# First units of a tile with attention turns between them, in a kernel of linear attention and two gated layers

## The chip, the cores and the metric

The kernel runs on one core of one Trainium2 chip. The metric is the device time of one execution in microseconds. The engines are named as the profile names them: PE is TensorE (matmul), PEld its weight loads, DVE VectorE, ACT ScalarE, SP SyncE, which here issues the DMAs, one behind the other in its own order.

## The reference

Random-feature attention on 4 batches of 8 heads, 576 tokens, 64 values a head (b h s d), with 128 features (m), then two layers over all 2304 tokens of 512 values:

```python
def phi(x):
    proj = np.einsum('bhsd,md->bhsm', x, omega)
    sq = np.sum(x * x, axis=-1, keepdims=True) / 2.0
    h = proj - sq
    h = h - np.max(h, axis=-1, keepdims=True)
    return np.exp(h) / np.sqrt(m)
q_p, k_p = (phi(q_s), phi(k_s))
kv = np.einsum('bhsm,bhsd->bhmd', k_p, v)
z = np.sum(k_p, axis=2)
num = np.einsum('bhsm,bhmd->bhsd', q_p, kv)
den = np.einsum('bhsm,bhm->bhs', q_p, z)[..., None] + 1e-06
attn_out = num / den
...
h = x @ w_in                                   # 512 -> 2048
x = (h * (1.0 / (1.0 + np.exp(-1.702 * h)))) @ w_out   # 2048 -> 512
...
a = x @ w_a                                    # 512 -> 1536
b = x @ w_b
return a * b @ w_out                           # 1536 -> 512
```

q_s and k_s are q and k by a constant. All is in float32.

## The kernel before

Most products are made of fp16 pairs: each float32 operand is split into a high and a low half, and high·high, high·low and low·high are summed, three matmuls for one product.

The first layer runs over five token tiles: one of 512 tokens for each batch, and one of 256 for the tokens left over. `ffn1` (L608 on) makes a tile of 16 units of 128 hidden values. A unit's h products are L623 to L625 (four chunks of 128 inputs, three matmuls of 512 columns each); then tanh on ACT (L631), `th` on DVE (L634), the high half `gh` on ACT (L640), the low half `gl` on DVE (L641); and the unit's 12 y products (L654 to L656) add into four accumulators, which are copied out at the tile's end (`ye`, ACT, L668) and stored. `main` runs y of unit f and then h of unit f + 2. The first units of a tile are made by `head`, before `main`: it issues the products of the first units on chunks 0 to 2, then, unit by unit, those on chunk 3 with all that follows. The input is xT; its chunk c is written by head pair c of the batch's attention, so that chunk 3 comes last.

Attention of one batch is a set of eight Python generators: four k phases (`kphase32`, L493; one pair of heads each) and four q phases (`qphase`, L513). A phase loads raw k or q, makes the fp16 pair x16 (ACT L394, DVE L395), transposes it by DMA into xt (L400), sums the squares (ACT L413 or L421, DVE L423), projects on omega (PE, L406 and L407), takes maxima (DVE L470) and small per-token terms (DVE L476), exponentials (ACT L437), and then the k phase forms kv (PE, L501 and L503). The q phase transposes the exponentials (PE L526, copied by ACT L528), multiplies by kv (PE L533), normalises (DVE L557 to L562, into xf), makes an fp16 pair again (ACT L595, DVE L596) and transposes it by DMA into xT (L603).

Weights arrive as raw chunks of 1 MB (`wraw`, L200, two buffers) and are split into halves by DVE (L214, L254, L262, L221) and ACT (L272), in steps: `w_steps(n, upto)` takes n of them, and one step issues the load of the chunk two further on.

The order of the program is written by four helpers. `begin_k` and `begin_q` put the phases into a list, each to start two turns behind the one before. `side_step` is one turn: every live phase goes on to its next yield. `run(gen, rate, wmax)` goes through a generator, and at each yield does `rate` steps of weight conversion and one turn. `finish_side` takes turns until no phase is left; `next_tile` calls it before the next tile is made. A scheduler then sets the order on each engine from dependencies and priorities, which follow the program's order. Attention of batch b runs beside tile b − 1 (its x is made by batch b − 1), and the q phase's end loads the next batch's k.

Batch 0's attention comes first, alone. Then `head(following[0], 3)` makes three units of tile 0 in one go (`following` is the list of tiles). Then, for b = 1, 2, 3: the phases of batch b are put on the list and the tile b − 1 is run with turns between. Behind batch 1's loop, `head(following[-1], 2)` makes two units of tile 1 in one go.

Of the kernel before, what the change touches and what calls it, by code (L numbers as in the profile page):

```python
# [33 lines left out]
def fused_kernel(  # L34
# [40 lines left out]
    first = ExitStack()  # L75
# [91 lines left out]
    NW1 = len(chunks)  # L167
# [117 lines left out]
    def w_steps(n, upto):  # L285
        for _ in range(n):
            if w_done[0] < upto:
                w_done[0] = next(w_gen)

    def w_need(n):  # L290
        while w_done[0] < n:
            w_done[0] = next(w_gen)
# [11 lines left out]
    def alloc_own(pool):  # L304


        own["ident"] = pool.tile([P, P], F32, name="ident", bufs=1)
        own["kv"] = pool.tile([P, NHP, 2, VC], F32, name="kv32", bufs=1)
        make_identity(nc, own["ident"])
        own["vt"] = vt = pool.tile([P, H, NT, VC], F32, name="vt", bufs=1)  # L310
        own["vm"] = vm = pool.tile([P, NHP, 2, VC], F32, name="vm", bufs=1)
        nc.gpsimd.memset(vt[:, :, :, D:VC], 1.0)
        nc.gpsimd.memset(vm, 0.0)
        for hh in range(2):
            nc.gpsimd.memset(vm[hh * SR : (hh + 1) * SR, :, hh, D:VC], 1.0)

    def prep(pool):
        om2 = stg.tile([P, 2, D], F32, tag="sx", name="om2", bufs=1)
        om = own["om"]
        for j in range(2):  # L320
            nc.vector.tensor_scalar(
                out=om2[:, j, :], in0=om, scalar1=QSCALE * S_OM, scalar2=None, op0=ALU.mult
            )
        pt = ps_att.tile([P, 512], F32, tag="att", name="pt")
        nc.tensor.transpose(pt[:, :P], om2.rearrange("p a b -> p (a b)"), own["ident"])
        nc.gpsimd.memset(om_f, 0.0)
        for j in range(2):
            nc.vector.tensor_copy(om_f[j * D : (j + 1) * D, j], pt[j * D : (j + 1) * D, :P])
        nc.scalar.copy(om_h, pt[:, :P])
        nc.vector.tensor_tensor(out=om_l, in0=pt[:, :P], in1=om_h, op=ALU.subtract)  # L330
# [6 lines left out]
    def a_load(pool, kind, b, hp):  # L337

        if b >= B or (kind, b, hp) in raws:
            return  # L340
        src = {"q": q, "k": k}[kind]
        h0 = 2 * hp
        place = kind
        if b == 0 and hp == NHP - 1:
            place = {"q": "k", "k": "q"}[kind]
        t = pool.tile([P, T, D], F32, tag=f"raw{place}", name=f"raw{kind}_{b}_{hp}", bufs=RAW[place])
        nc.sync.dma_start(
            out=t[:, 0 : 2 * NT, :].rearrange("p (h t) d -> p h (t d)", h=2),
            in_=src[b, h0 : h0 + 2, 0:SM, :].rearrange("h (p t) d -> p h (t d)", t=NT),
        )  # L350
        nc.sync.dma_start(out=t[:, 2 * NT, :], in_=src[b, h0 : h0 + 2, SM:S, :])
        raws[kind, b, hp] = t

    def v_load(b, part=None):
        if b >= B:
            return
        main = v[b, :, 0:SM, :].rearrange("h (p t) d -> p h t d", t=NT)
        for t in range(NT) if part is None else (part,):
            nc.sync.dma_start(out=own["vt"][:, :, t, 0:D], in_=main[:, :, t])
        for hh in (0, 1) if part is None else (part,) if part < 2 else ():  # L360
            nc.sync.dma_start(
                out=own["vm"][hh * SR : (hh + 1) * SR, :, hh, 0:D],
                in_=v[b, :, SM:S, :].rearrange("(n h) s d -> h s n d", h=2)[hh],
            )
# [633 lines left out]
    def side_step():  # L998

        while waiting and waiting[0][0] <= turn[0]:  # L1000
            live.append(waiting.pop(0)[1])
        for g in list(live):
            if next(g, live) is live:
                live.remove(g)
        turn[0] += 1
# [10 lines left out]
    def run(gen, rate, wmax):  # L1016

        due = 0.0
        for _ in gen:
            due += rate  # L1020
            if rate < 1:
                with tc.issue_after(own["nb"]):
                    w_steps(int(due), wmax)
            else:
                w_steps(int(due), wmax)
            due -= int(due)
            side_step()

    def finish_side():
        while waiting or live:  # L1030
            side_step()
# [7 lines left out]
    def begin_k(b, pool, psp, t0, lag, f32):  # L1039
        for hp in range(NHP):  # L1040
            def nx(hp=hp):
                if hp + 1 == NHP:
                    a_load(pool, "q", b, 0)

            begin(t0 + lag * hp, kphase32(pool, b, hp, psp, nx, f32))

    def begin_q(b, pool, xT, psp, t0, lag, f32):
        for hp in range(NHP):
            def nx(hp=hp):
                if hp + 1 < NHP:  # L1050
                    a_load(pool, "q", b, hp + 1)
                with tc.issue_after(own["xt", f"q{b}_{hp}"].ins):
                    a_load(pool, "k", b + 1, hp)
                if hp + 1 == NHP:
                    begin(0, v_parts(b + 1, own["xt", f"q{b}_{hp}"]))

            begin(t0 + lag * hp, qphase(pool, b, hp, xT, psp, nx, f32))

    def xparts(xT):
        return lambda c: xT[:, c, 0, :], lambda c: xT[:, c, 1, :]  # L1060

    def x_tile(b, pool, tag):
        return pool.tile([P, KC, 2, SM], F16, tag=tag, name=f"xT{b}")
# [4 lines left out]
    def fillers(n):  # L1068
        for _ in range(n):
            nc.tensor.matmul(  # L1070
                idle[:, 0:256].rearrange("p (r m) -> p r m", r=2), om_h,
                om_h[:, None, :].to_broadcast([P, 2, M]), start=True, stop=True,
            )
# [15 lines left out]
    following = []  # L1089

    def head(tile, units):
        _, products, unit = tile
        for f in range(units):
            w_need(2 * (f // RW) + 1)
            if f < 2:
                products(f, range(KC - 1))
            else:
                products(f, range(KC - 1), ps_acc, "acc")
        for f in range(units):
            unit(f, (KC - 1,))  # L1100

    def next_tile(make):
        def made():
            finish_side()
            following.append(make())
            return following[-1]

        return made

    xT = x_tile(0, zp, "z")  # L1110
    with tc.tile_pool(name="att", bufs=2) as att:
        own["om"] = att.tile([P, D], F32, tag="om", name="om", bufs=1)
        nc.scalar.dma_start(out=own["om"], in_=omega)
        a_load(att, "k", 0, 0)
        warm = att.tile([P, 1], F32, tag="warm", name="warm", bufs=1)
        nc.vector.memset(warm, 0.0)
        nc.scalar.activation(out=warm, in_=warm, func=AF.Exp)
        alloc_own(att)
        prep(att)
        fillers(1)  # L1120
        for hp in range(1, NHP):
            a_load(att, "k", 0, hp)
        w_steps(START_W, NW1)
        begin_k(0, att, psp_start, 0, LAG, True)
        begin_q(0, att, xT, psp_start, NHP * LAG, LAG, True)
        for n in range(VT):
            side_step()
        v_load(0)
        finish_side()
        fillers(FILL)  # L1130
        w_steps(POST_W, NW1)
        following.append(ffn1(0, *xparts(xT), SM))
        head(following[0], 3)
        for b in range(1, B):
            x1 = x_tile(b, zp, "z")
            begin_k(b, att, psp_att, 0, AL, b == 1)
            begin_q(b, att, x1, psp_att, NHP * AL, AL, b == 1)
            ahead = next_tile(lambda: ffn1(b, *xparts(x1), SM))
            if b == 1:
                run(following[-1][0](first=3), 1, NW1)  # L1140
                ahead()
                head(following[-1], 2)
            else:
                run(following[-1][0](ahead), 11 / 32, (NW1 + 2, NWE)[b - 2])
    late["pool"] = ctx.enter_context(tc.tile_pool(name="late", bufs=1))
    run(following[-1][0](next_tile(rest_tile)), 22 / 32, NW2)
# [48 lines left out]
```

## Time and profile before

| | |
|---|---|
| median of 3 runs | 915.58 us (915.47, 915.58, 917.74) |
| the profiled execution | 920.41 us |
| its span | 918.6 us |
| mean granted clock of TensorE | 0.994 |
| busy PE, PEld | 887.8 us (97%), 640.3 us (70%) |
| busy DVE, ACT | 678.5 us (74%), 440.2 us (48%) |
| y products, L655 | 115.2 us in 320, 4.7 us idle before them, by gl |
| h products, L623 | 97.9 us in 256, 4.3 us idle before them, 2.8 of it by xT |

Busy time is summed over the span. The profile was taken from one execution, and its span stands 1.8 us under that execution's time. Times in rows count from the start of the span; a group's idle time is that of its engine just before the group's instructions, with the releaser that ended most of it. Rows of TensorE overlap: a matmul's duration is longer than the time from its start to that of the next one. A row with "x22" stands for so many instructions, fp32 matmuls counting twice because they go through the array in two passes.

### The profile page before, as it was taken

The numbers are of one execution on the slowest core, as the hardware profiler recorded it, in microseconds if no ns is written. First come the engines' busy times: TensorE is split into PE (matmuls) and PEld (weight loads), VectorE is DVE, ScalarE is ACT, GpSimd is POOL, SyncE is SP. The second block draws the span as 40 slices with busy tenths as digits, with TensorE's granted clock in tenths as the row PEclk, the third lists the DMA queues.
The fourth block names the chain that finished last, engine by engine and source line by source line (L and its number), as shares of the span: only waits on it lengthen the run. The fifth ranks groups of instructions, "written<-read, shape, count | busy, mean of one in ns | idle before, by whom it ended". The sixth has DMA issues, their size and how long they took to land.

```text
span 918.6 us, 17124 instructions
## 1 busy us (share of the span) xinstructions
PE 887.8 (97%) x6984; PEld 640.3 (70%) x6984; DVE 678.5 (74%) x1220; ACT 440.2 (48%) x1047; POOL 1.7 (0%) x11
## 2 busy tenths in 40 slices
PE   7999989989999999999999999999999999999997
PEld 6864555645655456544447888888988888888886
DVE  5889988555779477899943379976999567566766
ACT  5656777554655566655423355443543232232221
POOL 0000000000000000000000000000000000000000
PEclk9999998999999999999999999999999999999999
DMA  7846686432475324773521043323330122223312
GB/s 178 222 129 193 201 211 177 140 62 72 115 155 137 92 61 66 133 215 127 211 92 46 1 145 101 124 103 118 131 127 16 67 42 81 81 93 127 76 47 70
DMA packets 129343, 105.35 MB, mean 115 GB/s; under 512 B 97776, under 2 KB 111088, under 8 KB 127216
## 3 DMA queue, kind: packets, MB, share of 16 engines
q1 hardware_dynamic: 128960, 103.96, 40.0%
q8 instruction: 55, 0.90, 0.4%
q10 hardware_dynamic: 304, 0.30, 0.1%
q14 instruction: 24, 0.20, 0.1%
HBM read 71.07 MB, written 17.69 MB: 97 GB/s over the span
## 4 chain that ended last, share of the span: by engine, by line
PE 65%; DVE 21%; ACT 6%; DMA 6%; issue 2%; SPq 1%; ACTq 0%; DVEq 0%
PE y L655 4%; PE y L656 4%; PE ph L623 4%; PE ph L625 4%; PE ph L624 4%; PE y L654 4%; PE pa L503 2%; PE oA L873 2%; PE oA L871 2%; PE oA L872 2%; PE pbA L778 2%; PE pbA L780 2%; PE pbA L779 2%; PE paA L778 2%; DVE wf L254 2%
## 5 line engine op out<-in xcount | busy, mean ns | idle before, releaser
L655 PE MATMUL y<-gl,w_out 128*128 128x512 f16 (+1 forms) x320 | 115.2, 361 | 4.7 <-DVE gl L641 4.7
L656 PE MATMUL y<-gh,w_out 128*128 128x512 f16 (+1 forms) x320 | 115.3, 361 | 0.0
L654 PE MATMUL y<-gh,w_out 128*128 128x512 f16 (+1 forms) x320 | 112.3, 358 | 0.1
L623 PE MATMUL ph<-xT,w_in 128*128 128x512 f16 x256 | 97.9, 382 | 4.3 <-DMA xT<-x_q_3x 2.8
L625 PE MATMUL ph<-xT,w_in 128*128 128x512 f16 x256 | 98.1, 383 | 0.6 <-DVE w_in L221 0.6
L624 PE MATMUL ph<-xT,w_in 128*128 128x512 f16 x256 | 97.6, 381 | 0.3 <-DVE xT L592 0.3
L634 DVE SCALAR_TENSOR_TENSOR th<-th,ph 128x512 f32<-128x512 f32 (+1 forms) x80 | 50.4, 630 | 47.9 <-ACT th L631 47.5
L631 ACT ACTIVATE th<-ph 128x512 f32<-128x512 f32 (+1 forms) x80 | 44.3, 553 | 62.6 <-PE ph L625 60.2
L640 ACT ACTIVATE gh<-th 128x512 f16<-128x512 f32 (+1 forms) x80 | 47.0, 588 | 52.3 <-DVE th L634 52.0
L641 DVE SCALAR_TENSOR_TENSOR gl<-th,gh 128x512 f16<-128x512 f32 (+1 forms) x80 | 50.6, 634 | 17.3 <-ACT gh L640 17.0
L778 PE MATMUL paA<-forms,w_a 128*128 128x256 f16 (+1 forms) x240 | 61.0, 262 | 1.6 <-DVE ca L797 0.8
L778 PE MATMUL pbA<-forms,w_b 128*128 128x256 f16 (+1 forms) x240 | 61.1, 262 | 1.0 <-DVE cb L797 1.0
L780 PE MATMUL pbA<-forms,w_b 128*128 128x256 f16 (+1 forms) x240 | 61.0, 262 | 0.0
L779 PE MATMUL pbA<-forms,w_b 128*128 128x256 f16 (+1 forms) x240 | 61.0, 262 | 0.0
L780 PE MATMUL paA<-forms,w_a 128*128 128x256 f16 (+1 forms) x240 | 61.0, 262 | 0.0
L779 PE MATMUL paA<-forms,w_a 128*128 128x256 f16 (+1 forms) x240 | 61.0, 262 | 0.0
L871 PE MATMUL oA<-w_o,ab 128*128 128x256 f16 x216 | 58.9, 273 | 1.6 <-ACT ab L829 0.9
L873 PE MATMUL oA<-w_o,ab 128*128 128x256 f16 x216 | 58.9, 273 | 0.6 <-DVE ab L830 0.5
L872 PE MATMUL oA<-w_o,ab 128*128 128x256 f16 x216 | 58.9, 273 | 0.0
L656 PEld LDWEIGHTS <-w_out 128*128 128x128 f16 x320 | 31.4, 98 | 35.2 <-issue 7.6
L624 PEld LDWEIGHTS <-w_in 128*128 128x128 f16 x320 | 31.7, 99 | 32.9 <-issue 6.1
L786 ACT COPY ka<-paA 128x512 f32<-128x512 f32 (+1 forms) x30 | 16.3, 544 | 78.2 <-PE paA L780 78.1
(195 smaller groups left out, 2317.5 us busy)
## 6 DMA issues: line engine op xcount, KB each, us to landing
wraw<-in_moe_w_out_dram SPq DMA_DIRECT2D x14, 1024.0 KB
forms<-fd SPq DMA_DIRECT2D x8, 1792.0 KB
wraw<-in_moe_w_in_dram SPq DMA_DIRECT2D x8, 1024.0 KB
fd<-forms SPq DMA_DIRECT2D x4, 1792.0 KB
wraw<-in_moe_w_a_dram SPq DMA_DIRECT2D x6, 1024.0 KB
wraw<-in_moe_w_b_dram SPq DMA_DIRECT2D x6, 1024.0 KB
rawk<-in_k_dram SPq DMA_DIRECT2D x16, 256.0 KB
vt<-in_v_dram SPq DMA_DIRECT2D x16, 256.0 KB
```

The costliest lines, as they stand in the source:

```text
L623: nc.tensor.matmul(ph[:, :n], w[:, 0, c, fs], xh(c), start=(c == 0), stop=False)
L624: nc.tensor.matmul(ph[:, :n], w[:, 0, c, fs], xl(c), start=False, stop=False)
L625: nc.tensor.matmul(ph[:, :n], w[:, 1, c, fs], xh(c), start=False, stop=(c == KC - 1))
L654: nc.tensor.matmul(o, w[:, 0, f % 4, cs], gh[f][:, :n], start=(f == 0), stop=False)
L655: nc.tensor.matmul(o, w[:, 0, f % 4, cs], gl[f][:, :n], start=False, stop=False)
L656: nc.tensor.matmul(o, w[:, 1, f % 4, cs], gh[f][:, :n], start=False, stop=(f == FC1 - 1))
L778: nc.tensor.matmul(o[:, i], wh, xh, start=first, stop=False, skip_group_check=True)
L779: nc.tensor.matmul(o[:, i], wh, xl, start=False, stop=False, skip_group_check=True)
L780: nc.tensor.matmul(o[:, i], wl, xh, start=False, stop=final, skip_group_check=True)
L871: nc.tensor.matmul(bank[:, t], lh, wh, start=first, stop=False, skip_group_check=True)
L872: nc.tensor.matmul(bank[:, t], lh, wl, start=False, stop=False, skip_group_check=True)
L873: nc.tensor.matmul(bank[:, t], ll, wh, start=False, stop=final, skip_group_check=True)
```

## The change

`head` becomes a generator with a yield behind each unit's first products and behind each unit. For batch 1, tile 0's head of three units is no longer issued ahead of the loop, but inside it, behind `begin_k` and `begin_q`, through `run` at one weight step and one turn a yield: six yields, six turns. Tile 1's head of two units moves from the end of the pass for b = 1 into that for b = 2, again behind `begin_k` and `begin_q`, through `run` at 11/32 weight steps a yield: four turns. The passes for b = 3 and for the rest stay.

```diff
                 products(f, range(KC - 1))
             else:
                 products(f, range(KC - 1), ps_acc, "acc")
+            yield
         for f in range(units):
             unit(f, (KC - 1,))
+            yield
...
         following.append(ffn1(0, *xparts(xT), SM))
-        head(following[0], 3)
         for b in range(1, B):
             x1 = x_tile(b, zp, "z")
             begin_k(b, att, psp_att, 0, AL, b == 1)
             begin_q(b, att, x1, psp_att, NHP * AL, AL, b == 1)
             ahead = next_tile(lambda: ffn1(b, *xparts(x1), SM))
             if b == 1:
-                run(following[-1][0](first=3), 1, NW1)
+                run(head(following[0], 3), 1, NW1)
+                run(following[0][0](first=3), 1, NW1)
                 ahead()
-                head(following[-1], 2)
             else:
+                if b == 2:
+                    run(head(following[-1], 2), 11 / 32, NW1 + 2)
                 run(following[-1][0](ahead), 11 / 32, (NW1 + 2, NWE)[b - 2])
```

How this moves instructions is shown at three places. In the order's names, `ph1_0` is tile 1's product of unit 0, `y0_1` tile 0's accumulator 1, `gh0_14` the high half of tile 0's unit 14, `xt_q1_2` the transposed q of batch 1, head pair 2; the numbers behind are the compiler's.

TensorE around the last attention product of batch 1 (L533, head pair 3), only matmuls' rows picked from the list, the weight loads (LDWEIGHTS) between them left away. The kernel before:

```order
L533 MATMUL pa_2084<-kv32_113,eT32_q1_3_2040 128x65 x4
L533 MATMUL pa_2084<-kv32_113,eT32_q1_3_2040 64x65 x2
L533 MATMUL pa_2120<-kv32_113,eT32_q1_3_2040 128x65 x5
L624 MATMUL ph1_1_2222<-xT1_911,w_in0_87 128x512
L625 MATMUL ph1_1_2222<-xT1_911,w_in0_87 128x512
L623 MATMUL ph1_0_2212<-xT1_911,w_in0_87 128x512
```

The same place in the changed kernel:

```order
L533 MATMUL pa_1966<-kv32_113,eT32_q1_3_1925 128x65 x4
L533 MATMUL pa_1966<-kv32_113,eT32_q1_3_1925 64x65 x2
L533 MATMUL pa_1995<-kv32_113,eT32_q1_3_1925 128x65 x5
L656 MATMUL y0_1_1011<-gh0_14_2134,w_out3_92 128x512
L654 MATMUL y0_2_1015<-gh0_14_2134,w_out3_92 128x512
L655 MATMUL y0_2_1015<-gl0_14_2135,w_out3_92 128x512
```

Before, tile 1's h products follow the last attention product at once, and the first on chunk 3 stands eight matmuls behind it. Now y products of tile 0's unit 14 follow, then those of unit 15 and tile 1's products on chunks 0 to 2: 37 matmuls up to the first on chunk 3.

SP's queue around the transposition of batch 1's second q, with the weight loads behind it. The kernel before:

```order
L200 DMA wraw12_1648<-in_moe_w_in_dram 128x4x512
L400 DMA_TRANSPOSE xt_q1_1_1398<-x16_q1_1_1395 128x9x128
L347 DMA rawk_2_1_1442<-in_k_dram 128x2x256
L351 DMA rawk_2_1_1442<-in_k_dram 128x1x64
L200 DMA wraw13_1700<-in_moe_w_out_dram 128x2x1024
L200 DMA wraw14_1883<-in_moe_w_in_dram 128x4x512
```

The same place in the changed kernel:

```order
L200 DMA wraw9_1467<-in_moe_w_out_dram 128x2x1024
L200 DMA wraw10_1642<-in_moe_w_in_dram 128x4x512
L400 DMA_TRANSPOSE xt_q1_1_1283<-x16_q1_1_1280 128x9x128
L347 DMA rawk_2_1_1324<-in_k_dram 128x2x256
L351 DMA rawk_2_1_1324<-in_k_dram 128x1x64
L200 DMA wraw11_1696<-in_moe_w_out_dram 128x2x1024
L400 DMA_TRANSPOSE xt_q1_2_1394<-x16_q1_2_1391 128x9x128
```

The transposition `xt_q1_1` was followed by weight chunk 13 and is now followed by chunk 11; chunk 9 follows `xt_q1_0`, chunk 12 follows `xt_q1_2` and chunk 13 follows `xt_q1_3`, in the same way.

SP's queue at the end of tile 0: stores of y, the last transpositions of batch 1's output into xT, the loads of k of batch 2, head pair 3, and its first transposition `xt_k2_0`. The kernel before:

```order
L669 DMA yd0_2199<-ye0_3_2209 128x512
L603 DMA_TRANSPOSE xT1_911<-x16_q1_1x_1994 128x8x128
L603 DMA_TRANSPOSE xT1_911<-x16_q1_2x_2078 128x8x128
L603 DMA_TRANSPOSE xT1_911<-x16_q1_3x_2148 128x8x128
L400 DMA_TRANSPOSE xt_k2_0_2273<-x16_k2_0_2270 128x9x128
L347 DMA rawk_2_3_1671<-in_k_dram 128x2x256
L351 DMA rawk_2_3_1671<-in_k_dram 128x1x64
```

The same place in the changed kernel:

```order
L603 DMA_TRANSPOSE xT1_841<-x16_q1_3x_2028 128x8x128
L669 DMA yd0_2199<-ye0_1_2203 128x512
L669 DMA yd0_2199<-ye0_2_2206 128x512
L669 DMA yd0_2199<-ye0_3_2209 128x512
L347 DMA rawk_2_3_1553<-in_k_dram 128x2x256
L351 DMA rawk_2_3_1553<-in_k_dram 128x1x64
L400 DMA_TRANSPOSE xt_k2_0_2227<-x16_k2_0_2224 128x9x128
```

The first transposition of batch 2 stood ahead of the loads of `rawk_2_3` and now stands behind them and behind three stores of y.

## Rows read from the trace of the kernel before

**Rows 1.** Busy time of each engine by stretch: us, PE PEld DVE ACT POOL, PEclk, DMA, GB/s.

```profile
59.00:192.00 133.00, 124.33 (x754) 68.96 (x751) 110.80 (x194) 85.25 (x300) 0.00 (x0) 0.97 0.61 170
...
60.00:120.00 60.00, 56.64 (x323) 29.08 (x322) 58.38 (x89) 40.40 (x152) 0.00 (x0) 1.00 0.63 183
...
138.00:144.00 6.00, 5.99 (x15) 2.08 (x15) 4.18 (x7) 4.99 (x25) 0.00 (x0) 0.51 0.47 116
...
195.00:199.00 4.00, 4.00 (x21) 2.28 (x20) 2.39 (x4) 3.28 (x6) 0.00 (x0) 0.57 0.78 171
...
200.00:918.00 718.00, 704.29 (x5844) 522.57 (x5841) 522.30 (x909) 311.17 (x624) 0.00 (x0) 1.00 0.34 98
```

**Rows 2.** Timeline of TensorE, mid-tile: start, us, instruction, [idle before].

```profile
138.01 0.59 PE L655 MATMUL y<-gl,w_out 128*128 128x512 f16 x1 [2.74 <-DVE gl L641]
...
143.93 0.38 PE L624 MATMUL ph<-xT,w_in 128*128 128x512 f16 x1
```

**Rows 3.** Chain of waits, 120 to 205 us: start, us, what.

```profile
123.71 1.96 SPq L400
...
127.02 7.57 DMA wraw<-in_moe_w_out_dram
134.61 0.70 DVE wf L214
...
137.36 0.61 DVE gl L641
```

**Rows 4.** Timeline of TensorE: matmuls and projections one behind another.

```profile
66.74 0.38 PE L623 MATMUL ph<-xT,w_in 128*128 128x512 f16 x1
66.96 0.38 PE L624 MATMUL ph<-xT,w_in 128*128 128x512 f16 x1
...
80.65 0.22 PE L406 MATMUL pa<-om_h,xt_k 128*128 128x128 f16 x1
80.70 0.22 PE L407 MATMUL pa<-om_l,xt_k 128*128 128x128 f16 x1
```

**Rows 5.** Timeline of TensorE, end of tile 0.

```profile
181.38 2.63 PE L533 MATMUL pa<-kv,eT_q 128*128 128x65 f32 x22 [0.54 <-ACT eT_q L528]
...
185.11 0.74 PE L526 MATMUL pa<-ident,e_q 128*128 128x128 f32 x5 [0.62 <-DVE xf_q L562]
...
186.54 2.53 PE L533 MATMUL pa<-kv,eT_q 128*128 128x65 f32 x22
...
190.54 0.38 PE L623 MATMUL ph<-xT,w_in 128*128 128x512 f16 x1 [1.04 <-DMA xT<-x_q_2x]
...
194.76 0.38 PE L623 MATMUL ph<-xT,w_in 128*128 128x512 f16 x1 [2.76 <-DMA xT<-x_q_3x]
...
198.60 0.38 PE L624 MATMUL ph<-xT,w_in 128*128 128x512 f16 x1
```

**Rows 6.** Chain of waits, 120 to 205 us, end of tile 0.

```profile
191.47 3.25 DMA xT<-x_q_3x
```

**Rows 7.** Timeline of VectorE, early in tile 0.

```profile
83.82 0.75 DVE L395 SCALAR_TENSOR_TENSOR x_k<-rawk,x_k 128x576 f16<-128x576 f32 x1
84.49 0.15 DVE L476 SCALAR_TENSOR_TENSOR nb_k<-mh_k,sq_k 128x4 f32<-128x4 f32 x1
...
86.30 0.68 DVE L470 TENSOR_REDUCE mx_k<-pa 128x4 f32<-128x512 f32 x1
86.90 1.21 DVE L221 SCALAR_TENSOR_TENSOR w_out<-wf,w_out 128x1024 f16<-128x1024 f32 x1
88.03 0.69 DVE L641 SCALAR_TENSOR_TENSOR gl<-th,gh 128x512 f16<-128x512 f32 x1
```

**Rows 8.** Timeline of ScalarE, VectorE and SP's queue, end of tile 0.

```profile
177.52 1.12 ACT L668 ACTIVATE ye<-y 128x512 f32<-128x512 f32 x2
...
193.30 0.75 DVE L423 TENSOR_REDUCE sq_k<-rawk 128x9 f32<-128x576 f32 x1 [0.75 <-ACT rawk L421]
...
194.21 0.53 SPq L347 DMA_DIRECT2D rawk<-in_k_dram  x1
```

## The prediction

> **What bounds the kernel now.** I read the busy times by stretches first, then TensorE's own timeline through tile 0, then the chain of waits behind the longest wait, and last the order of instructions. From 200 us on TensorE is busy 704.29 of 718 us at full clock [rows 1]: little is to be won there, and what is won ahead of it stays won, since that part does the same work. The stretch from 59 to 192 us holds tile 0 and batch 1's attention; TensorE is busy 124.33 of 133 us, VectorE 110.80. VectorE is nearly full only in the first half of it (58.38 of 60 us from 60 to 120). So TensorE sets the pace of the whole, with stalls in tile 0, and VectorE comes close behind it early on.
>
> The stalls are two. **Mid-tile**: at 138.01 a product of y waits 2.74 us for gl [rows 2]. The chain leads back from gl at 137.36 to wf at 134.61, to the load of a weight chunk issued at 127.02 that took 7.57 us, to a transposition on SP's queue at 123.71 that stood ahead of it [rows 3]. The wait is followed by a granted clock of 0.51 from 138 to 144 us [rows 1], the 1.2 GHz level. Between 138.01 and 143.93 [rows 2] lie 14 products of 512 columns; at full clock one follows the other in 66.96 − 66.74 = 0.2157 us (unrounded) [rows 4], so 3.02 us of work took 5.92. The stall costs 2.74 + 2.90 = 5.64 us.
>
> **End of tile 0**: TensorE waits 0.54, 0.62, 1.04 and 2.76 us [rows 5], together 4.96. The last two are for the transpositions that bring batch 1's output into xT. From 194.98 (0.22 after the row at 194.76) to 198.60 the clock is low again (0.57 from 195 to 199 [rows 1]): 7 products of 512 columns and 12 projections took the 3.84 us from 194.76, where 7 × 0.2157 + 12 × 0.055 (80.70 − 80.65 [rows 4]) = 2.17 would do. So 1.67 lost, 6.63 in all. Both stalls make **12.27 us**, all that the change can well take away.
>
> **The change, part by part.** No multiplication, copy or load is added or taken away; TensorE has two rows more in the order and VectorE one, from other grouping, which I cost at nothing.
>
> *Six turns ahead of tile 0's main loop.* Batch 1's attention starts during units 0 to 2 of the tile instead of behind them, and six steps of weight conversion go with it. It therefore ends some six turns sooner: at its last product the order has 7 + 12 products of y and 18 of the next tile's h still to issue ahead of that tile's first use of xT's chunk 3, so 37 × 0.2157 = 8.0 us. Before, it had 8, 1.7 us. What the chunk needs is the time from the end of that product (186.54 + 2.53) to 194.76 [rows 5]: 5.7 us, 3.25 of it the transposition [rows 6]. 8.0 covers 5.7, so the waits of 1.04 and 2.76 and the low clock behind them go. The two of 0.54 and 0.62 lie within the attention, which now has y products between its steps; they can come back there. Gain 6.63, less what follows.
>
> *The mid-tile stall.* VectorE's duties stand against TensorE's. I count the instructions in the order up to each unit's gl (VectorE) and up to its first use (TensorE), each by its spacing. VectorE's rows overlap: an instruction's spacing is its duration less 0.08 (83.82 + 0.75 − 84.49 [rows 7]). Before unit 6's gl stand one L214 more (0.70 [rows 3], so 0.62), one L221 and one L262 (1.13 each, 88.03 − 86.90), two L395 (0.67), four maxima of L470 over four groups (0.60, 86.90 − 86.30) and three over one group (a third of that, an estimate), and nine small L476 (0.15 − 0.08): 0.62 + 2.26 + 1.34 + 2.40 + 0.60 + 0.63 = 7.9, with the unrounded spacings **8.0 us**. TensorE gets 5 products, 36 projections and 18 products in fp32 more: 1.08 + 1.98 + 18 × 2 × 0.108 (the 2.53 of 22 passes, less 0.16 for the last one's latency, by 22 [rows 5]) = 6.95, with the few rows between 7.1. So unit 6 is **0.9 us tighter**. By unit 10 it is VectorE +2.1 against TensorE +4.2, by unit 12 +1.7 against +5.9: 4.2 us looser where the stall was. The wait of 2.74 fits into it, so 5.64 goes, if the load comes no later against the work than now.
>
> *Queues.* SP's order changes. Weight loads 9, 11, 12 and 13 now stand each behind a transposition of q that waits for its buffer; before, 12, 13, 15 and 16 did. Load 13 has batch 2's loads of v ahead of it too. I take the same wait as at 123.71 for each, hidden by the 4 us that VectorE gained. If that cover is gone, the wait of rows 2 is back.
>
> *Tile 1's first two units.* They move behind batch 2's first four turns. TensorE's cover for the first transposition xt_k2_0 is 46 products, 9.9 us after the last product of batch 1. It is ready after the sum at 193.30 + 0.75, which is 5.0 after that product's end, three copies of y (1.12 for two, 1.7 in all), two loads issued at 0.53 each, 1.2 with their gaps [rows 8], and 3.3 for the transposition and its landing [rows 6]: 11.2. A new wait of **1.3 us**, from 0 (the loads don't hold it) to 3.3 (none of the transposition is covered).
>
> *Steps of the q chain within the last units*: the trace does not show them there. Nearest are 0.54 and 0.62 [rows 5]; I take 1.0 for both kinds, from 0 to 2. The tighter units 3 to 6: 0.9, from 0 to 2 (each row of the count lies between 0.3 and 1.8).
>
> Sum: −12.27 + 1.3 + 1.0 + 0.9 = **−9.1 us**, from −12.3 to −5.0. The profiled execution, 920.41, would come to 911.3. It stands 4.83 above the median of the runs, 915.58, and I subtract the same from that: 906.4.
>
> **A rule against it.** The spacing of 0.2157 us [rows 4] is what makes TensorE the bound: 384 products of one tile take 82.8 us, and attention comes beside them. The Trainium skill, "TensorE: Matmul & The Clock Gate", section "Back-to-back issue gap", gives about 131 ns for such a product in a sustained stream of weight loads and matmuls. By it the 384 take 50.3 us, VectorE would be the bound of the tile, and starting attention earlier would win nothing: the second rival. No row of this trace shows that spacing, so by the trace the rule does not hold here.
>
> **The rivals.**
> *A. The weight load keeps its stall, at another unit.* For it: four loads stand behind transpositions [rows 3], now earlier chunks than before, which earlier units want. Against it: 4.2 us of room at unit 12. Then 5.64 stays: −12.27 + 3.2 + 5.64 = −3.4, 912.2. That timed runs lie 4.83 under the profiled one, so that one of the two stalls may be smaller in them, would look the same.
> *B. VectorE takes the gain.* For it: 58.38 of 60 us busy up to 120 us [rows 1], and 8.0 us more work in front of unit 6. If TensorE's 7.1 us, which feed on VectorE's results, can't be done in the meantime, all 8.0 is waited for: −12.27 + 8.0 + 1.3 + 1.0 = −2.0, 913.6: no difference that can be told. Against it: over the whole stretch VectorE is busy 110.80 us, and even 133 − 12.3 = 120.7 would be left for it. It decides when VectorE has no idle time left up to unit 10.
> *C. Slower: SP's queue.* Loads 9, 11 and 12 too come late behind the transpositions, and the mid-tile stall comes three times instead of once, each with its low clock: −12.27 + 3.2 + 3 × 5.64 = +7.9, 923.5. It decides when a transposition waits so long that the load behind it lands over 4 us later against VectorE's work than the one of rows 3. For it: one load is enough for 5.64 [rows 2, 3]. Against it: two staging buffers let each load run ahead by one chunk. The Trainium skill, "DMA: Bandwidth & Descriptors", section "Anatomy of one DMA — SWDGE (gpsimd) path", has the waits of a DMA stand on the issuing sequencer ahead of its dispatch, though it says so for GpSimd's path; the row at 123.71 agrees for SP's.
>
> **How the numbers follow.** A measurement of this kernel can tell about 0.3%, 2.75 us: 912.8 to 918.3 is no change. Forecast 0.55 (906.4, its own range 903.2 to 910.6), A 0.22, B 0.14, C 0.09. The small waits elsewhere in the stretch (133 − 124.33 less the named ones that lie in it) could give 1 us more: low end 902. Leaving out C and a little of the tails, the range goes up to B: 914. Faster by over 0.3%: 0.55 and most of A, 0.75; no change: B and the rest, 0.17; slower: 0.08.
>
> **What would show it.** Right: no wait over 1.5 us for xT at the end of tile 0 and none over 1 us for gl in mid-tile; full clock from 66 us to tile 1; a small wait for xt_k at the start of tile 1; tile 1's first products about 9 us sooner. A: a wait of 2 to 3 us for gl or w_out with low clock, its chain ending in a weight load. B: many small waits for gl in units 3 to 9 and VectorE over 97% busy up to 120 us. C: two or more such waits as in A. The prediction is wrong if the sum of TensorE's idle time and low clock up to 200 us falls by less than 5 us, or if the time that comes after 200 us changes by over 2 us.

## The result and the profile after

The changed kernel takes 910.13 us (median of 6 runs, 909.17 to 911.17), the kernel before in the same comparison 918.66 (6 runs, 915.47 to 922.72): a ratio of 0.9908, 95% interval 0.988 to 0.9937. A second comparison on another chip gave 910.7 against 917.7, 0.9927 (0.9902 to 0.9951); 8 to 9 us had been expected of it, and 7.0 came. So it is faster, by 0.7 to 0.9%; the time lies in the range that was forecast (902 to 914), 3.7 us above the forecast itself. The profiled execution takes 911.17 us against 920.41.

Busy time by stretch of the changed kernel, columns as in [rows 1]:

```profile
59.00:192.00 133.00, 126.30 (x783) 70.96 (x782) 117.14 (x204) 89.54 (x298) 0.00 (x0) 1.00 0.67 176
...
60.00:120.00 60.00, 55.26 (x346) 30.43 (x344) 56.57 (x95) 44.43 (x171) 0.00 (x0) 1.00 0.70 183
...
120.00:145.00 25.00, 24.95 (x159) 13.99 (x158) 23.09 (x40) 17.10 (x68) 0.00 (x0) 1.00 0.99 249
...
200.00:909.00 709.00, 694.96 (x5784) 517.77 (x5781) 514.30 (x894) 303.87 (x607) 0.00 (x0) 1.00 0.34 99
```

Against [rows 1], TensorE's clock is full throughout, and from 120 to 145 us, where the mid-tile stall stood, it is busy 24.95 of 25 us. From 60 to 120 it is busy less than before (55.26 against 56.64): something is lost early. From 200 us to the end it lacks 14.04 us, where it lacked 13.71 [rows 1]: the part behind tile 0 is as it was.

The groups of the page that had idle time, again with the idle time and its releaser at the end of the row:

```profile
L655 PE MATMUL y<-gl,w_out 128*128 128x512 f16 (+1 forms) x320 | 114.3, 358 | 0.7 <-DVE gl L641 0.7
L654 PE MATMUL y<-gh,w_out 128*128 128x512 f16 (+1 forms) x320 | 112.5, 358 | 2.1 <-ACT gh L640 1.9
L623 PE MATMUL ph<-xT,w_in 128*128 128x512 f16 x256 | 97.1, 379 | 2.4 <-DMA xT<-x_q_3x 1.4
```

L655 waited 4.7 us, by gl, and now 0.7; L623 waited 4.3 and now 2.4, of which 1.4 stand in a later tile; L654 has 1.9 new, for gh.

TensorE's timeline at the end of tile 0, from the last attention product of batch 1 to tile 1:

```profile
174.43 2.63 PE L533 MATMUL pa<-kv,eT_q 128*128 128x65 f32 x22
176.90 0.38 PE L656 MATMUL y<-gh,w_out 128*128 128x512 f16 x1
...
184.89 0.38 PE L623 MATMUL ph<-xT,w_in 128*128 128x512 f16 x1
...
187.16 0.38 PE L623 MATMUL ph<-xT,w_in 128*128 128x512 f16 x1 [0.82 <-DVE th L634]
...
188.77 0.23 PE L406 MATMUL pa<-om_h,xt_k 128*128 128x128 f16 x1 [0.80 <-DMA xt_k<-x_k]
```

The last product (174.43) is followed by 37 matmuls, and 184.89 is the first one on chunk 3 of xT: 7.99 us after 176.90, at the spacing of [rows 4], with no wait where the kernel before waited 1.04 and 2.76 [rows 5]. The waits of 0.54 and 0.62 inside the attention are gone too. Two new ones stand at the start of tile 1: 0.82 for th and 0.80 for xt_k. When chunk 3 landed shows on ScalarE, whose next fp16 copy waited for the same transposition:

```profile
183.54 0.68 ACT L394 ACTIVATE x_k<-rawk 128x576 f16<-128x576 f32 x1 [0.88 <-DMA xT<-x_q_3x]
```

So xT was complete by 183.5, 1.4 us ahead of its use.

And early in tile 0, the two longest waits that the kernel before did not have:

```profile
72.88 0.81 PE L654 MATMUL y<-gh,w_out 128*128 128x512 f16 x3 [1.93 <-ACT gh L640]
...
84.86 0.22 PE L406 MATMUL pa<-om_h,xt_k 128*128 128x128 f16 x1 [1.56 <-ACT e_k L437]
```

A second execution of the changed kernel was profiled, with the same program. The later of these two waits is there again (1.55); the earlier one is only 0.62 us, in TensorE's timeline:

```profile
71.80 0.81 PE L654 MATMUL y<-gh,w_out 128*128 128x512 f16 x3 [0.62 <-ACT gh L640]
```

### The profile page after: what moved, and what is told of

Its sections match the earlier page's. It is cut to its first block, busy times and chain, and to the rows that moved or that the text cites. A ratio compares the mean times of both kernels' runs of the same rounds, so it can differ in the third digit from the quotient of the medians.

```text
span 909.3 us, 17130 instructions
## 1 busy us (share of the span) xinstructions
PE 884.1 (97%) x6984; PEld 639.5 (70%) x6984; DVE 676.9 (74%) x1220; ACT 439.3 (48%) x1047; POOL 1.7 (0%) x11
## 4 chain that ended last, share of the span: by engine, by line
PE 67%; DVE 19%; ACT 7%; DMA 4%; issue 2%; SPq 1%; ACTq 0%; DVEq 0%
PE y L654 4%; PE y L655 4%; PE y L656 4%; PE ph L623 4%; PE ph L624 4%; PE ph L625 3%; PE pa L503 3%; PE oA L873 2%; DMA xt_k<-x_k 2%; PE oA L871 2%; PE oA L872 2%; PE pbA L778 2%; PE pbA L780 2%; PE pbA L779 2%; PE pa L533 2%
## 5 line engine op out<-in xcount | busy, mean ns | idle before, releaser
L655 PE MATMUL y<-gl,w_out 128*128 128x512 f16 (+1 forms) x320 | 114.3, 358 | 0.7 <-DVE gl L641 0.7
L654 PE MATMUL y<-gh,w_out 128*128 128x512 f16 (+1 forms) x320 | 112.5, 358 | 2.1 <-ACT gh L640 1.9
L623 PE MATMUL ph<-xT,w_in 128*128 128x512 f16 x256 | 97.1, 379 | 2.4 <-DMA xT<-x_q_3x 1.4
L879 DVE SCALAR_TENSOR_TENSOR o<-oA,o 128x512 f32<-128x512 f32 (+1 forms) x45 | 28.5, 633 | 34.5 <-PE oA L873 34.5
```

The costliest lines, as they stand in the source:

```text
L623: nc.tensor.matmul(ph[:, :n], w[:, 0, c, fs], xh(c), start=(c == 0), stop=False)
L654: nc.tensor.matmul(o, w[:, 0, f % 4, cs], gh[f][:, :n], start=(f == 0), stop=False)
L655: nc.tensor.matmul(o, w[:, 0, f % 4, cs], gl[f][:, :n], start=False, stop=False)
```

## The experiments

Two theories stood against each other for each stall. For the end of tile 0: batch 1's attention is ready sooner (tile 0's head), or batch 2's turns fill the wait (tile 1's head). For mid-tile: the attention is sooner, or the weights are converted and loaded sooner.

**One half of the change alone (e1, e2).** Tile 0's head with turns, tile 1's in one go:

```diff
-                    run(head(following[-1], 2), 11 / 32, NW1 + 2)
...
                 ahead()
+                for _ in head(following[-1], 2):
+                    pass
```

> Only tile 0's head gives turns; tile 1's head is issued in one go again. Theory (both stalls of the kernel before end because batch 1's attention starts six turns sooner): the waits of 2.74 for gl in mid-tile and of 1.04 and 2.76 for xT at the end of tile 0 are gone, and with them 12.3 us, less the two new waits early in tile 0 (1.9 and 1.6 in the changed kernel, about 2.4 us more than what stood there): 9 to 10 us faster than before, within 1 us of the full change. Rival (the end of tile 0 is cured by batch 2's turns between tile 1's first units): the waits of 1.04 and 2.76 and the low clock stay, some 3 us faster only.

Measured: 910.84 against 918.11 us, 0.9918 (0.9896 to 0.994), so 7.3 us faster, less than the 9 to 10 expected and beside 8.5 and 7.0 for the whole change. In its profile the waits for gl and for xT are gone; the longest wait from 55 to 215 us is 1.55 us. The rival falls.

The other half (e2), tile 0's head in one go ahead of the loop:

```diff
+        for _ in head(following[0], 3):
+            pass
...
-                run(head(following[0], 3), 1, NW1)
```

> Only tile 1's head gives turns, with batch 2; tile 0 as before. Theory: both stalls stay, since batch 1's attention is no earlier; 0 to 1.5 us slower or faster than before (a wait for xt_k2_0 of up to 1.3 us comes, some work may fill the waits for xT). Rival: the 6.6 us at the end of tile 0 go, the wait in mid-tile stays.

Measured: 915.98 against 918.11 us, 0.9978 (0.996 to 0.9997): some 2 us faster, more than expected. But both stalls stand, as the theory has it, in its timeline of TensorE:

```profile
138.22 0.59 PE L655 MATMUL y<-gl,w_out 128*128 128x512 f16 x1 [3.08 <-DVE gl L641]
...
190.09 0.38 PE L623 MATMUL ph<-xT,w_in 128*128 128x512 f16 x1 [0.66 <-DMA xT<-x_q_2x]
...
194.71 0.54 PE L623 MATMUL ph<-xT,w_in 128*128 128x512 f16 x1 [3.16 <-DMA xT<-x_q_3x]
```

Where the 2 us come from was not found out: the execution that was profiled, at a mean clock of 0.994, is as long (920.36) as that of the kernel before (920.41). Tile 0's head alone (0.9918) makes the whole gain (0.9908 and 0.9927); what tile 1's half adds to it can't be told from these runs.

**Turns without weight steps (e3), and steps without turns (e4).** Tile 0's head at no weight step a yield:

```diff
-                run(head(following[0], 3), 1, NW1)
+                run(head(following[0], 3), 0, NW1)
```

> The full change, but without the six weight conversion steps in tile 0's head: turns alone. Theory (it is the attention's start that matters): as fast as the full change within 1.5 us, no stall in mid-tile and none for xT. Rival (the weights converted and loaded six steps sooner cured the mid-tile stall): a wait of 2 to 3 us for gl with a low clock behind it is back, 5 to 6 us slower than the full change, about 3 us faster than before.

Measured: 908.94 against 918.11 us, 0.9898 (0.9877 to 0.992). Neither stall is there; what's more, neither are the early waits of 1.93 and 1.56: the longest wait from 55 to 215 us is 0.80. So the turns are enough for the gain, and the six weight steps that came with them make the early loss. In the same comparison e1, which has the steps (and tile 1's head in one go), stands at 910.84.

The other way round, six steps between the yields and no turn:

```diff
-        head(following[0], 3)
+        for _ in head(following[0], 3):
+            w_steps(1, NW1)
```

(`head` with its yields; tile 1's head in one go.)

> The kernel before with six weight conversion steps between tile 0's first units and no turns there. Theory: no difference to before that can be told (within 1.5 us): both stalls stay. Rival (earlier conversion cures the mid-tile stall): 5.6 us faster, no wait over 1 us for gl.

Measured: 919.25 against 918.11 us, 1.0015 (0.9999 to 1.0031): no gain. The end of tile 0 waits 1.22 and 2.65 us for xT. The wait for gl has shrunk to 0.25, with 1.45 for th in its place:

```profile
135.85 0.38 PE L623 MATMUL ph<-xT,w_in 128*128 128x512 f16 x1 [1.45 <-DVE th L634]
...
137.79 0.38 PE L655 MATMUL y<-gl,w_out 128*128 128x512 f16 x1 [0.25 <-DVE gl L641]
```

There is an early wait of 1.70 too that the kernel before doesn't have. So the rival is half right: steps alone take the wait for gl away as well, but VectorE still waits 2.18 us for the weight load, the wait turns up at another place, and nothing is won by it.

**The low clock behind a wait (e7).** The kernel before, with 20 matmuls that nobody reads ahead of tile 1's first product on chunk 3:

```diff
-    def head(tile, units):
+    def head(tile, units, dummy=None):
...
+        if dummy is not None:
+            for _ in range(20):
+                nc.tensor.matmul(
+                    dummy[:, 0:256].rearrange("p (r m) -> p r m", r=2), om_h,
+                    om_h[:, None, :].to_broadcast([P, 2, M]), start=True, stop=True,
+                )
         for f in range(units):
             unit(f, (KC - 1,))
...
-                head(following[-1], 2)
+                dummy = psp_att()
+                head(following[-1], 2, dummy)
```

> The kernel before, with 20 matmuls of 256 columns that nothing reads (each 0.11 us, 2.2 in all) issued on TensorE ahead of tile 1's first product on chunk 3, in the wait of 2.76 us. Theory (TensorE's half clock behind the wait comes from its standing idle, and is worth 1.67 us): the wait for xT shrinks to about 0.6 us, the clock stays at its full level from 195 to 199 us, and runs at a mean clock of 0.994 or 0.995 are gone; median 1 to 2 us faster than before. The mid-tile stall stays. Rival (the low clock has another cause): it stays between 195 and 199 us, no difference.

Measured: 916.28 against 917.7 us, 0.9984 (0.9967 to 1.0001). The wait that was 2.76 [rows 5] is 1.18 us in TensorE's timeline:

```profile
193.13 0.38 PE L623 MATMUL ph<-xT,w_in 128*128 128x512 f16 x1 [1.18 <-DMA xT<-x_q_3x]
```

And by stretch, the clock from 195 to 199 us is full where it was 0.57 [rows 1]:

```profile
195.00:199.00 4.00, 4.00 (x24) 1.90 (x22) 4.00 (x8) 2.96 (x6) 0.00 (x0) 1.00 0.43 84
```

All its 12 runs have a mean granted clock of 0.998 to 1.000, where those of the kernel before go down to 0.993. That fits the theory, and the gain of the median (1.4 us) is as large as forecast, but its interval just touches no difference. Nor is it shown that the added matmuls did it: in the same profile the clock from 138 to 144 us is higher too (0.72, where it was 0.51 [rows 1]), some 50 us ahead of them, and e4 and e12 have full clock behind waits of 2.65 and 3.17 us that nothing fills.

**The weight load behind the mid-tile wait (e11, e12).** First, chunk 13's load issued on ScalarE's queue:

```diff
-            nc.sync.dma_start(out=t, in_=src)
+            (nc.scalar if i == 13 else nc.sync).dma_start(out=t, in_=src)
```

> The kernel before, with the one weight load behind the mid-tile wait (chunk 13, issued at 127.02) on ScalarE's queue, where it waits only for its own buffer (free when L262 ends at 125.5). Theory (the load is late because SP held it behind the transposition and two loads of k): it is issued about 1.5 us sooner, the wait of 2.74 for gl falls to 0.5 to 1.5 us, and the low clock from 138 to 144 us goes or is rarer: 1.5 to 4 us faster; the end of tile 0 stays as it was. Rival (the transfer's 7.6 us, slowed by the other transfers, sets it, wherever it is issued): the wait stays at 2.5 or more, no difference to before.

Measured: 922.07 against 919.23 us, 1.0036 (1.0022 to 1.0051), slower. The expectation missed: on ScalarE the load stands behind exponentials that wait for TensorE, and it goes out later, not sooner. The timeline of ScalarE's DMA issues:

```profile
131.13 0.40 ACTq L200 DMA_DIRECT2D wraw<-in_moe_w_out_dram  x1
```

and that of VectorE, where the load is waited for:

```profile
140.75 0.69 DVE L214 TENSOR_SCALAR wf<-wraw 128x1024 int32<-128x1024 int32 x1 [6.70 <-DMA wraw<-in_moe_w_out_dram]
```

It is issued 4.1 us later than at 127.02 [rows 3], and VectorE waits 6.70 us for it, where it waited 2.61 in the kernel before:

```profile
134.61 0.69 DVE L214 TENSOR_SCALAR wf<-wraw 128x1024 int32<-128x1024 int32 x1 [2.61 <-DMA wraw<-in_moe_w_out_dram]
```

The run is a dose all the same: the later load is passed on to VectorE in full.

Then (e12) the other way: two loads of k on ScalarE's queue, which lets SP take chunk 13 ahead of the transposition.

```diff
-        nc.sync.dma_start(
+        eng = nc.scalar if (kind, b, hp) == ("k", 2, 1) else nc.sync
+        eng.dma_start(
```

(The second load of a_load likewise.)

> The kernel before, with the two loads of k for batch 2, head pair 1 on ScalarE's queue; the load of weight chunk 13 then stands on SP's queue ahead of the transposition of q1_1 instead of behind it, and waits only for its own buffer, which is free when L262 ends at 125.5. Theory (the mid-tile stall is this load's lateness, passed on by VectorE): it is issued about 1.5 us sooner than at 127.02, VectorE's wait of 2.61 for it falls by as much, TensorE's wait of 2.74 for gl falls to 0.5 to 1.7, and the low clock behind it is rarer: 1 to 4 us faster. The waits at the end of tile 0 stay, by the changed order of the transpositions perhaps 1 us later. Rival (VectorE's own work up to gl sets the wait, the load only comes last by chance): the wait for gl stays at 2.3 or more.

Measured: 917.87 against 917.61 us, 0.9992 (0.9975 to 1.0009): no difference. In its profile the load is issued at 119.62, 7.4 us sooner (1.5 had been expected), since VectorE frees its buffer sooner too: the L262 before it starts at 118.38, where it started at 124.31. VectorE's wait for the load falls from 2.61 to 0.84 us, and TensorE's wait for gl is gone. SP's timeline:

```profile
119.62 0.37 SPq L200 DMA_DIRECT2D wraw<-in_moe_w_out_dram  x1
```

By stretch, TensorE loses little from 120 to 145 us, at full clock, but it loses more behind tile 0:

```profile
55.00:200.00 145.00, 135.47 (x835) 76.13 (x834) 120.92 (x213) 96.18 (x323) 0.00 (x0) 1.00 0.63 164
...
120.00:145.00 25.00, 23.83 (x159) 13.90 (x158) 22.99 (x39) 19.94 (x73) 0.00 (x0) 1.00 0.86 224
...
200.00:520.00 320.00, 312.65 (x2068) 174.54 (x2067) 223.92 (x462) 163.47 (x375) 0.00 (x0) 1.00 0.44 109
```

The same stretches of the kernel before:

```profile
55.00:200.00 145.00, 133.53 (x813) 75.54 (x812) 118.70 (x209) 92.30 (x315) 0.00 (x0) 0.96 0.60 164
...
200.00:520.00 320.00, 315.14 (x2063) 174.11 (x2061) 226.27 (x467) 166.48 (x381) 0.00 (x0) 1.00 0.43 109
```

Up to 200 us TensorE's idle time falls from 11.47 to 9.53, 1.9 us; from 200 to 520 it grows from 4.86 to 7.35 (6.19 in the kernel before, profiled once more, below). So the cause of the mid-tile wait is shown (the load behind the transposition), and its worth isn't: the median stayed where it was, a gain of 2.3 us at the most by the interval, against 5.64 in the sum, but behind tile 0 e12 loses most or all of what it gains in it. The end of tile 0 still waits 0.71 and 3.17 for xT, which comes no sooner behind the attention's end.

**The kernel before, once more.**

> The kernel before, profiled once more, to see which of its stalls stand in every execution. Theory (the waits are of the program's order and stay; the low clock behind them comes in some executions only and makes the spread): waits of 2 to 3 us for gl near 138 and of 4.5 to 5.5 us in all at the end of tile 0 are there again, within 0.5 us; the low clock may be absent at either place, and the execution is shorter by what of it is absent (up to 4.6 us). Rival (the waits themselves vary, with the speed of the transfers): one of the two is shorter by over 1.5 us.

The profiled waits are the same within 0.3 us: 2.70 for gl, 0.53, 0.62, 0.78 and 3.04 at the end of tile 0, 4.97 in all against 4.96. The low clock came at both places again (0.59 from 138 to 144, 0.68 from 195 to 199). Over the experiments' comparisons there are 91 executions of the kernel before with a mean granted clock each. The 20 at 0.999 or 1.000 have a median of 916.09 us, 39 at 0.996 to 0.998 one of 917.41, and 32 at 0.993 to 0.995 one of 920.34. So both profiles, which are of executions at 0.994, have the same waits; the low clock comes in some executions and not in others, and 4.3 us lie between. That the waits are the same in executions at full clock is likely, but none of those was profiled. Of the changed kernel 12 executions lie between 909.17 and 911.47, all at 0.999 or 1.000.

**Can the new costs be had back (e8, e9, e10)?** Turns without steps, and the load of rawk_2_3 moved into the first k phase:

```diff
+                if b > 1 and hp == 0:
+                    a_load(pool, "k", b, NHP - 1)
...
-                with tc.issue_after(own["xt", f"q{b}_{hp}"].ins):
-                    a_load(pool, "k", b + 1, hp)
+                if b == 0 or hp + 1 < NHP:
+                    with tc.issue_after(own["xt", f"q{b}_{hp}"].ins):
+                        a_load(pool, "k", b + 1, hp)
```

> Turns without weight steps as in e3, and from batch 2 on the load of the fourth k (rawk_2_3) is issued within the first k phase, so that SP does not hold the first transposition xt_k2_0 behind it. Theory (xt_k2_0 is late by SP's queue, as forecast): the wait of 0.76 us before L406 at the start of tile 1 is gone, 0.5 to 1 us faster than e3. Rival (a buffer of the fp16 pairs holds the turn up on ScalarE, through the wait for the transposition of x_q_3x): the wait of 0.8 for th at the start of tile 1 stays and that for xt_k too, within 0.3 us of e3.

Measured: 908.37 us, beside 910.7 for the changed kernel and 917.7 for the kernel before in the same comparison, 0.9904 (0.9877 to 0.993) of the latter. Its six executions (907.8 to 909.3) all lie below the six of the changed kernel (909.8 to 911.47). The transposition of xt_k2_0 goes out 1.5 us sooner than in e3 (180.84 against 182.30), yet the projection waits 0.86 us for it, at an earlier place in TensorE's order; it is the wait for th that is gone. This version beats both kernels. That the load's move adds to it isn't shown: e3, without the move, came to 0.9898 of the kernel before on another chip, and the 0.5 to 1 us expected on top of e3 did not come.

Then (e9) three buffers for the fp16 pairs, paid for with one of raw q, on top of e3:

```diff
-    RAW = {"k": 3, "q": 4}
+    RAW = {"k": 3, "q": 3}
...
-            x16 = pool.tile([P, T, 2, D], F16, tag="A", name=f"x16_{nm}")
+            x16 = pool.tile([P, T, 2, D], F16, tag="A", name=f"x16_{nm}", bufs=3)
```

(All tiles of that tag.)

> Turns without weight steps as in e3, and three buffers instead of two for the fp16 pairs (x16), paid for with three instead of four buffers of raw q. Theory (two buffers of x16 let ScalarE stand before a transposition has read one, and units stand behind it): the wait of 0.8 us for th at the start of tile 1 goes, 0.5 to 1.5 us faster than e3. Rival (SP's queue alone delays xt_k2_0; the buffers don't matter, or the third raw q buffer is missed): same as e3, or slower by up to 2 us.

Measured: 909.89 us, 0.9922 (0.9895 to 0.9948) of before. The wait for th stays (0.76), that for xt_k too (0.67), and a new one of 1.77 for th stands at 128.62. So the buffers weren't what held tile 1's start: in ScalarE's order the fp16 copies and squares of the next batch stand ahead of the tile's first tanh.

Last (e10), e8 with tile 0's stores on ScalarE's queue:

```diff
-                        nc.sync.dma_start(out=yd[:, c, :n], in_=ye[:, :n])
+                        (nc.scalar if j == 0 else nc.sync).dma_start(out=yd[:, c, :n], in_=ye[:, :n])
```

> e8 with tile 0's four stores of y issued from ScalarE's queue instead of SP's, so that xt_k2_0 on SP stands behind no store. Theory (SP's queue sets when xt_k2_0 starts): it starts 1.3 to 1.6 us sooner (behind x_q_3x's transposition and DVE's L395), the wait of 0.86 before L406 goes, 0.3 to 0.9 us faster than e8. Rival (xt_k2_0 waits for ScalarE's fp16 copies, which the stores' issue now delays): the wait stays or grows, 0 to 1 us slower than e8.

Measured: 908.59 against 919.23 us, 0.9889 (0.9865 to 0.9912): no better than e8. The transposition starts 2.3 us sooner than in e8 and is done later. The chain of waits:

```profile
178.51 7.17 DMA xt_k<-x_k
```

and TensorE's timeline at its use:

```profile
185.73 0.29 PE L406 MATMUL pa<-om_h,xt_k 128*128 128x128 f16 x1 [2.37 <-DMA xt_k<-x_k]
```

It took 7.17 us beside the stores (issued from 176.97 to 180.49) and beside the transposition of x_q_3x (176.75 to 181.17); in e8, where the other landed as it started, it took 3.77. Which of the two slowed it isn't shown. TensorE waited 2.37 and the clock fell behind that (0.72 from 184 to 190). The rival had the growing wait, though not for this reason.

## Why the prediction was right

**The stalls.** Both went, as forecast: 2.74 for gl, 4.96 at the end of tile 0, and the low clock behind them. The cover of 37 matmuls measured 7.99 us (forecast 8.0), and the landing of chunk 3 some 6.4 us after the last product's end (183.5 − 177.06; forecast 5.7). That it is batch 1's sooner attention, e1, e2 and e3 show.

For mid-tile the outcome was right, and the reason only in part. The prediction counts 4.2 us of room for VectorE at unit 12, "where the stall was". The gl that came late is that of unit 10, the eleventh in VectorE's order (units are counted from 0); there the prediction's own count gives 4.2 − 2.1 = 2.1 us, less than the 2.74. What else the traces show is VectorE's order: before, the L214 that waits for chunk 13 (134.61) stands ahead of this gl, which starts at 137.28; in the changed kernel the gl of unit 10 stands ahead of that L214 (143.99, shown under the rivals), which comes two units later, just ahead of unit 12's. VectorE's row of this gl, and TensorE's first product on it:

```profile
139.57 0.68 DVE L641 SCALAR_TENSOR_TENSOR gl<-th,gh 128x512 f16<-128x512 f32 x1
```

```profile
140.39 0.38 PE L655 MATMUL y<-gl,w_out 128*128 128x512 f16 x1
```

So gl is done 0.1 us before its use: no room of microseconds is seen at this unit, but it no longer stands behind the weight load. That the reordering is what saved it, and not the room, is argued from these rows; no run separates the two.

**The sum.** On the profiled execution −9.1 was forecast and 920.41 − 911.17 = 9.24 measured. That it fits to 0.1 us is luck: the second profiled executions, 920.85 and 909.91, are 10.94 apart, and two misses cancel in the first. By span and busy time TensorE is idle 918.6 − 887.8 = 30.8 us before and 909.3 − 884.1 = 25.2 after, 5.6 less (2.74 + 4.96 − 3.2 = 4.5 was forecast); its busy time is 3.7 less, which the low clock accounts for (2.90 + 1.67 = 4.57 was reckoned).

**The new costs**: 3.2 forecast. The wait for xt_k2_0 was put at 1.3 and is 0.80, with 0.82 for th beside it that was not foreseen; the copy was ready 11.7 us after the last product (188.73 − 177.06; forecast 11.2). The waits of the q chain were put at 1.0 and are not there. The early units were put at 0.9, for VectorE's work in units 3 to 6. There the waits did not grow; the loss is at unit 0 (1.93) and at a k phase (1.56), and 2.4 us of older small waits are gone in exchange, so that about 1.1 is left. In the second profile 0.62 and 1.55 stand there, and nothing is left. So its size was about right in one execution and too large in the other, and its place and engine were wrong: it is ScalarE that stands. The chain of waits of the changed kernel:

```profile
64.46 6.12 DMA xt_k<-x_k
...
70.68 0.68 ACT x_k L394
71.36 0.95 ACT w_out L272
72.31 0.53 ACT gh L640
...
72.88 0.81 PE y L654 x3
```

The fp16 copy at 70.68 waits for a transposition to free its buffer, and the weight step's L272 and then gh stand behind it in ScalarE's order. In the second profile the same transposition, issued at the same place, took 4.80 us, 1.3 less, and the wait is 1.3 shorter. The prediction counted VectorE's and TensorE's instructions and not ScalarE's. Without the weight steps (e3) the wait is gone.

**Where it was off: the step from the profiled execution to the runs.** The forecast lies 3.7 us under the measured time, mostly by one step: "It stands 4.83 above the median of the runs, 915.58, and I subtract the same from that: 906.4." The 4.83 were no constant: they are about the low clock itself, 4.57 by the reckoning of the same text, which the change takes away. The profiled execution was one of those with a low clock at both places; two of the three runs shown (915.58 and 915.47; their clock is not on record) would stand among the ten or eleven shortest of the 91, and the changed kernel has none of it. Subtracted only from the time before, 906.4 (915.58 − 9.1 is 906.5) should have been 911.3, the forecast for the profiled execution; 910.1 and 910.7 were measured. Rival A's last sentence named the possibility (a stall smaller in the timed runs), but gave it no time of its own. That the time lies in the range all the same, the width of the range did, not this step.

**What the mid-tile stall is worth** stays open in part. At full clock the gain is 916.09 − 910.1 = 6.0 us, close to the 5.6 us of idle time; e12, without the mid-tile wait, gains nothing at full clock either (its six executions at 0.999 or 1.000 have a median of 916.57), but it has 2.5 us more of idle time from 200 to 520 us (1.2 more than the second profile of the kernel before), which the changed kernel has not. So e12 does not price the wait. No execution of the kernel before at full clock was profiled, so what stands there isn't shown.

**The rivals.** A: the wait for a weight load did not come back; chunk 13's conversion begins at 143.99 without a wait, though its load goes out only at 135.18, behind v's. That is 8.8 us after the load's issue; before, the load took 7.57 [rows 3]. SP's timeline:

```profile
135.18 1.13 SPq L200 DMA_DIRECT2D wraw<-in_moe_w_out_dram  x1
```

VectorE's, a row without a wait:

```profile
143.99 0.69 DVE L214 TENSOR_SCALAR wf<-wraw 128x1024 int32<-128x1024 int32 x1
```

B: VectorE is busy 56.57 of the 60 us up to 120, less than before, and does not set the end; the spacing of matmuls is 0.22 again, so that TensorE stays the bound. The rule of the Trainium skill ("TensorE: Matmul & The Clock Gate", section "Back-to-back issue gap") by which it would not be is not borne out: no stretch here shows its 131 ns. C: no load came late enough; e11 shows what one such load costs in the kernel before, 2.8 us for a load that is 4.1 us later.

## What to carry to other kernels

Starting the next batch's work between a tile's first units pays at the tile's end, if the next tile's input is then ready before it is wanted: find the last producer, count the cover in instructions from there to the use, and compare it with the latency that the trace shows. Move only what has to be early: here the attention's turns had to; the weight steps that rode along only added waits. When room is counted for a late load, look up first which instruction stands behind the load in each engine's order, before and after. And before a sum is carried from one profiled execution to the timed runs, ask whether the difference between the two is the very thing that the change removes.

## What was not expected of the hardware

The DMA transposition of the same 128x9x128 tile took 3.23 us at 78.84 in the changed kernel, 4.14 behind two loads of k (184.59), 6.12 with a weight load of 1 MB issued 1.7 us ahead of it (64.46), and 7.17 beside four stores and another transposition (e10). The second profile has 4.80 at the place of the 6.12, with the same load ahead, so that the neighbours alone do not give the time. In e10 the transposition was issued 2.3 us sooner and landed later. And waits of 2.65 and 3.17 us for xT (e4, e12) were followed by full clock in their profiles, while in the profiles of the kernel before 2.76 and 3.04 were followed by half of it: as long a wait may or may not have the low clock behind it.
